# Scores of 64 attention units in plain float32 on half of TensorE's rows, in place of split operands on all rows

## The chip, the cores and the metric

The kernel runs on one core of a Trainium2 chip. A core has a matrix engine (TensorE, PE in the profile; PEld is its weight loading), VectorE (DVE), ScalarE (ACT), GpSimd (POOL) and SyncE (SP), which here issues the DMAs. Each engine runs its own list of instructions in order and waits for others through semaphores. Data lies in SBUF (128 partitions) and in PSUM, the output of TensorE, in eight banks of 512 float32 columns. The metric is the time of one execution on the device in microseconds (us).

## What is computed

Blockwise causal attention over q, k and v of 8 batches, 8 heads, 576 positions and 64 dimensions, and a feed-forward network on the result, all in float32:

```python
scores = scale * np.matmul(q, k.transpose(0, 1, 3, 2))  # scale = 1/8
mask = (pos[:, None] // 64) >= (pos[None, :] // 64)
scores = np.where(mask, scores, -1e9)
attn = np.exp(scores - scores.max(-1, keepdims=True))
attn = attn / (attn.sum(-1, keepdims=True) + 1e-9)
x = (attn @ v).transpose(0, 2, 1, 3).reshape(4608, 512)
h = x @ w_in                                                    # 512 x 2048
out = (h / (1 + np.exp(-h))) @ w_out                            # 2048 x 512
```

## The kernel before

**Float32 from a faster type.** TensorE takes plain float32 and float32r, a shorter type. Most matmuls here are float32r: an operand is split into a part `hi`, its cast to float32r, and a part `lo`, the rest, and a product is the sum of hi x hi, hi x lo and lo x hi. ScalarE does most of the casts and GpSimd the subtractions for `lo`.

**Units.** The first 128 query positions are handled early by other classes (`First`, L494, and `Second`, L551), whose scores are plain float32 matmuls with 64 rows of TensorE: `First.scores` at L526 uses four tiles of 64 rows by 64 output columns, one in each quarter, `Second.scores` at L578 two, one in the upper left and one in the lower right quarter. The other 448 queries of each of the 64 pairs of batch and head are a `Unit` (L263). A unit's keys are five tiles of 128, 128, 128, 128 and 64 positions; `SEG` (L40) has for each its number, its first column in the score buffer, its first query and how many queries see it: 448, 320, 192, 448 and 64 for the tiles 0, 2, 3, 1 and 4. `BANKS` (L45) puts tile 0 into PSUM bank 0, tiles 2 and 3 into bank 1, tiles 1 and 4 into bank 2.

**Steps of a unit, and their lines.** `load` (L269) brings q and k, transposed, with 64 dimensions as partitions, into the buffer `qkraw` twice by two DMAs, on partitions 0 to 63 and 64 to 127. `split_hi` (L278, ScalarE at L280) casts all of it to float32r into `qh`. `split_lo` (L282) overwrites the keys of `qh` on the partitions 64 to 127 by their rest (GpSimd, L284) and writes the rest of the queries to `ql` (GpSimd, L286). `scores` (L297) then contracts over all 128 partitions, so that one matmul adds the products with both parts of the keys: for each key tile two matmuls at L308, one with the queries' `qh` and one with `ql`, ten in all. `max` and `max2` (VectorE) find the maxima, `sub` subtracts them into the buffer `T`, `exp`, `p_hi` and `p_lo` make the weights and split them, `pv` (L382, matmuls at L387) multiplies with v, whose split `v_hi` and `v_lo` make, and `sums`, `lower`, `fold`, `mult`, `x_hi` and `x_lo` norm the result and split it into the FFN's input.

**FFN.** Blocks of 256 tokens: `ffn1` (L620) multiplies with w_in, `silu`, `g_hi` and `g_lo` (ScalarE, ScalarE, GpSimd) make the next operand, `ffn2` (L660) multiplies with w_out, all in float32r over 128 rows and 128 columns of TensorE.

**Order.** The schedule is written by hand. Up to unit 16 the string `ORDER` (L52) lists every step, a token like `u3.scores` being the method of unit 3 and `ffn` half a step of the FFN; from unit 17 on the loop at L760 does the same by rule: in its step i it issues the scores, `max` and `max2` of unit i, the splits of unit i+1, the load of unit i+2, some FFN, `pv` of unit i-1, and so on. Between a unit's matmuls TensorE always has FFN matmuls. SyncE issues all loads and stores in this order as well; a load waits until the buffer's former user is done. Every buffer named here exists once, so `qkraw` of unit i+2 is free when the splits of unit i+1 are done.

Of the kernel before, what the change touches and what calls it, by code (L numbers as in the profile page):

```python
# [9 lines left out]
F32 = mybir.dt.float32  # L10
F32R = mybir.dt.float32r
# [3 lines left out]
ALU = mybir.AluOpType  # L15
# [5 lines left out]
P = 128  # L21
NQ = S - 2 * D
# [17 lines left out]
SEG = [(0, 0, 0, 448), (2, 448, 128, 320), (3, 768, 256, 192), (1, 960, 0, 448), (4, 1408, 384, 64)]  # L40
COLS = 1472

QK = [0, 1, 3, 2, 4]
PV = [(0, 0, 128), (1, 0, 128), (2, 0, 128), (2, 1, 64), (1, 1, 64), (0, 1, 64), (4, 0, 128), (3, 1, 64), (3, 0, 128)]
BANKS = [(0, 448), (448, 960), (960, 1472)]  # L45

# [40 lines left out]
u2.sums u2.p_lo:2 u4.scores u1.mult g_lo u3.exp:0 ffn u3.exp:1 u4.max u5.split_hi u2.v_lo ffn u3.exp:2 u3.load_v u5.split_lo
u1.x_hi u3.sums u2.pv ffn silu u4.max2 u1.x_lo g_hi u6.load u2.lower ffn u3.p_hi:0 g_lo u3.v_hi u2.fold ffn u4.sub u3.v_lo silu
ffn u3.p_lo:0 u3.p_hi:1 u4.load_v g_hi u3.sums2 u3.p_hi:2 u3.p_lo:1 u5.scores u3.p_lo:2 ffn u4.exp:0 u5.max u6.split_hi g_lo u3.pv
u4.exp:1 u4.exp:2 u6.split_lo u5.max2 ffn u4.p_hi:0 u3.lower ffn u4.p_hi:1 u4.p_hi:2 u3.fold u4.p_lo:0 u7.load u5.sub ffn  # L90
u4.p_lo:1 silu ffn g_hi u3.mult u4.v_hi g_lo u6.scores u4.sums u3.x_hi u4.v_lo silu ffn u4.p_lo:2 u6.max u7.split_hi u5.load_v
store ffn u3.x_lo u6.max2 u4.pv u5.exp:0 u7.split_lo u5.exp:1 u5.exp:2 ffn u5.v_hi u5.sums u5.p_hi:0 u4.lower ffn u5.p_lo:0
u5.p_hi:1 u8.load u5.p_hi:2 u4.fold ffn g_hi u5.p_lo:1 u6.sub ffn u5.p_lo:2 u5.sums2 u6.exp:0 u7.scores u5.v_lo u6.exp:1 u6.exp:2
g_lo u6.load_v ffn u7.max u8.split_hi u5.pv u8.split_lo u7.max2 silu ffn g_hi u5.lower ffn u6.p_hi:0 g_lo u5.fold u9.load u6.v_hi
u7.sub u6.p_hi:1 ffn u6.v_lo silu u6.p_lo:0 g_hi ffn u7.load_v u5.mult u6.p_hi:2 g_lo u8.scores u6.sums u5.x_hi u6.p_lo:1 silu ffn
u9.split_hi u8.max u6.p_lo:2 ffn u5.x_lo u8.max2 u7.exp:0 u6.pv u7.exp:1 u9.split_lo u7.exp:2 ffn output g_hi u7.sums u7.v_hi ffn
u6.lower g_lo u7.p_hi:0 u10.load output u6.fold ffn u7.p_hi:1 u8.sub u7.p_lo:0 u7.p_hi:2 ffn u7.p_lo:1 u7.sums2 u9.scores
u7.p_lo:2 u8.exp:0 u8.exp:1 ffn u7.v_lo u9.max u8.exp:2 u10.split_hi u8.load_v u7.pv u10.split_lo u9.max2 ffn silu u7.lower ffn
# [34 lines left out]
def attn_ffn(ctx: ExitStack, tc: tile.TileContext, qk, v, qk0, v0, qk1, v1, w_in, w_out, out):  # L133
    nc = tc.nc
    pool = lambda name, bufs=1, **kw: ctx.enter_context(tc.tile_pool(name=name, bufs=bufs, **kw))
    cp = pool("const")
    sp = pool("work")
# [125 lines left out]
    class Unit:  # L263
# [3 lines left out]
            u.b, u.h, u.a = b, h, 64 * (h % 2)  # L267

        def load(u):  # L269
            u.raw = sp.tile([P, 1024], F32, tag="qkraw", name="qkraw")  # L270
            for r in (0, 64):
                nc.sync.dma_start(out=u.raw[r : r + 64], in_=qk[u.b, u.h])

        def load_v(u):
            u.vraw = sp.tile([P, 512], F32, tag="vraw", name="vraw")[:, : 5 * D]
            nc.sync.dma_start(out=u.vraw, in_=v[u.b, u.h])

        def split_hi(u):  # L278
            u.qh = sp.tile([P, 1024], F32R, tag="qh", name="qh")
            nc.scalar.copy(u.qh, u.raw)  # L280

        def split_lo(u):  # L282

            nc.gpsimd.tensor_tensor(out=u.qh[64:, NQ:], in0=u.raw[64:, NQ:], in1=u.qh[64:, NQ:], op=ALU.subtract)  # L284
            u.ql = sp.tile([P, 512], F32R, tag="ql", name="ql")[:, :NQ]
            nc.gpsimd.tensor_tensor(out=u.ql, in0=u.raw[:, :NQ], in1=u.qh[:, :NQ], op=ALU.subtract)  # L286
# [10 lines left out]
        def scores(u):  # L297
            banks = [bank(0), bank(1), bank(2)]

            def ps(c, w, r=P):  # L300
                i = max(i for i in range(3) if BANKS[i][0] <= c)
                return banks[i][:r, c - BANKS[i][0] : c - BANKS[i][0] + w]

            u.ps = ps
            for j, c, q0, w in (SEG[i] for i in QK):
                m = min(P, S - j * P)
                for i, qq in enumerate((u.qh, u.ql)):
                    nc.tensor.matmul(u.ps(c, w, m), u.kk[:, j * P : j * P + m], qq[:, q0 : q0 + w], start=i == 0, stop=i == 1)  # L308
# [118 lines left out]
    HALF = (slice(0, 64), slice(64, 128))  # L427
# [308 lines left out]
    units = [Unit(b, h) for b in range(B) for h in range(H)]  # L736
# [3 lines left out]
    a, b = First(0), First(1)  # L740
# [7 lines left out]
    for token in ORDER.split():  # L748
        name, _, method = token.partition(".")
# [10 lines left out]
    for i in range(TABLE, n + 2):  # L760
        u = units[i] if i < n else None
# [82 lines left out]
```

## Time and profile before

| | |
|---|---|
| median of 2 runs | 1041.92 us (1041.03 and 1042.81) |
| span of the profiled execution | 1040.4 us; its own total time is not given apart from the two runs |
| granted clock of TensorE | 1.000 |
| L308 to L308, scores of one unit to those of the next | some 12.7 us from 310 us on |
| DMA, mean over the span | 77 GB/s |

The profile is one execution recorded by the hardware. Times are microseconds from the start of the span, unless marked ns. L308 is line 308 of the kernel. In rows of groups stand the line, engine, operation, output and inputs by the program's names, the shapes, how many there were, then their busy time and the mean ns of one, then the idle time before them and what ended it. "128*64" is the part of TensorE used, rows by columns. In rows of the timeline stand the start, the time from the first start to the last end, and the count of like instructions merged. A plain float32 matmul shows as two weight loads and two matmuls. The ends of matmuls are modelled, and they overlap; their starts are recorded.

### The profile page before, as it was taken

How to read it: one execution, taken by the hardware profiler on the slowest of the kernel's cores; microseconds unless marked ns; L12 is line 12 of the kernel's file. 1: busy time of each engine (PE TensorE's matmuls, PEld its weight loads, DVE VectorE, ACT ScalarE, POOL GpSimd, SP SyncE). 2: the span in 40 equal slices, each digit the busy share in tenths (PEclk: the TensorE clock that was granted, in tenths of full speed). 3: DMA queues.
4: the chain of work that ended last, by engine and by line, in shares of the span. 5: the costliest groups of instructions: out<-in, count | busy, mean ns of one | idle time of the engine just before them, and what ended most of it. 6: DMA issues, size and time to landing. Idle time of an engine off the chain costs nothing.

```text
span 1040.4 us, 20218 instructions
## 1 busy us (share of the span) xinstructions
PE 1032.7 (99%) x7162; PEld 938.7 (90%) x7162; DVE 762.8 (73%) x2233; ACT 745.9 (72%) x1192; POOL 750.0 (72%) x726
## 2 busy tenths in 40 slices
PE   8999999999999999999999999999999999999998
PEld 8888899999999999999999999998999999989987
DVE  7998499999968988888878888888888888700000
ACT  4876498888987888787878787878787777722222
POOL 5775679988997878787878787878787878622221
PEclk9999999999999999999999999999999999999999
DMA  7865232232222222232222222222222222000000
GB/s 264 280 212 198 75 97 74 71 87 67 65 71 74 54 55 74 54 81 59 82 56 75 59 75 54 65 64 54 75 55 74 55 74 55 25 3 21 1 21 21
DMA packets 35188, 79.95 MB, mean 77 GB/s; under 512 B 4752, under 2 KB 13200, under 8 KB 35088
## 3 DMA queue, kind: packets, MB, share of 16 engines
q1 hardware_dynamic: 35088, 78.66, 27.2%
q8 instruction: 57, 0.93, 0.4%
q14 instruction: 43, 0.35, 0.1%
HBM read 69.21 MB, written 9.44 MB: 76 GB/s over the span
## 4 chain that ended last, share of the span: by engine, by line
PE 89%; POOL 4%; DVE 3%; DMA 1%; issue 1%; ACT 1%; SPq 0%; POOLq 0%; DVEq 0%; ACTq 0%
PE h L620 36%; PE o L660 36%; PE S L308 8%; PE U L387 8%; POOL pl L363 1%; DMA qk<-in_qk_dram 1%; PE S L660 1%; DVE wm L235 1%; PE S L578 1%; POOL qh L284 1%; DMA wst<-in_moe_w_out_dram 1%; POOL g L638 1%; DVE S L229 0%; POOL ql L286 0%; DVE S L225 0%
## 5 line engine op out<-in xcount | busy, mean ns | idle before, releaser
L620 PE MATMUL h<-x,wi 128*128 128x256 f32 x3456 | 441.0, 282 | 0.3 <-POOL x L424 0.3
L620 PEld LDWEIGHTS h<-x,wi 128*128 128x128 f32 x3456 | 430.0, 188 | 11.5 <-issue 0.5
L660 PE MATMUL o<-wo,g 128*128 128x512 f32 (+1 forms) x1680 | 423.9, 397 | 0.0
L660 PEld LDWEIGHTS o<-wo,g 128*128 128x128 f32 x1680 | 305.7, 188 | 62.6 <-issue 0.7
L363 POOL TENSOR_TENSOR pl<-p,ph 128x448 fp32r<-128x448 f32 (+1 forms) x192 | 226.0, 1202 | 92.9 <-ACT ph L355 92.9
L638 POOL TENSOR_TENSOR g<-g,g 128x512 fp32r<-128x512 f32 x144 | 186.4, 1294 | 120.3 <-ACT g L633 110.1
L252 DVE TRANSPOSE_TENSOR_REDUCE Mx<-S 64x4 f32<-64x128 f32 (+4 forms) x384 | 135.5, 405 | 92.9 <-PE S L308 92.7
L627 ACT ACTIVATE g<-h 128x512 f32<-128x512 f32 x144 | 86.1, 598 | 124.0 <-POOL g L638 76.3
L633 ACT CAST g<-g 128x512 fp32r<-128x512 f32 x144 | 89.3, 620 | 58.8 <-PE o L660 56.8
L252 DVE TRANSPOSE_TENSOR_REDUCE Dx<-p 128x14 f32<-128x448 f32 (+3 forms) x320 | 122.5, 445 | 0.1
L349 ACT ACTIVATE p<-T 128x512 f32<-128x512 f32 (+1 forms) x192 | 105.2, 604 | 14.8 <-POOL ph L365 13.8
L355 ACT CAST ph<-p 128x512 fp32r<-128x512 f32 (+1 forms) x192 | 104.1, 596 | 1.3 <-PE U L387 1.2
L284 POOL TENSOR_TENSOR qh<-qkraw,qh 64x576 fp32r<-64x576 f32 x64 | 91.8, 1434 | 16.6 <-ACT qh L280 7.7
L672 DVE TENSOR_TENSOR ot<-S,ot 128x256 f32<-128x256 f32 x1 | 0.4, 424 | 125.3 <-PE S L660 125.3
L308 PE MATMUL S<-qh 128*128 128x448 f32 (+3 forms) x320 | 91.1, 298 | 0.0
L627 ACT ACT_TABLE_LOAD x65 | 83.4, 1283 | 1.2
L308 PE MATMUL S<-ql,qh 128*128 128x448 f32 (+3 forms) x320 | 84.0, 307 | 0.0
L349 ACT ACT_TABLE_LOAD x61 | 78.3, 1283 | 1.3 <-DVE Dx L252 0.2
L286 POOL TENSOR_TENSOR ql<-qkraw,qh 128x448 fp32r<-128x448 f32 x64 | 74.1, 1158 | 5.0
L387 PE MATMUL U<-ph,vc 128*128 128x448 f32 (+3 forms) x320 | 74.0, 296 | 0.3 <-POOL vc L295 0.3
L340 DVE TENSOR_TENSOR T<-S,MR 128x256 f32<-128x256 f32 (+2 forms) x192 | 72.8, 405 | 0.0
L280 ACT CAST qh<-qkraw 128x1024 fp32r<-128x1024 f32 x64 | 66.9, 1045 | 7.3 <-DMA qkraw<-in_qk_dram 4.8
(121 smaller groups left out, 1175.3 us busy)
## 6 DMA issues: line engine op xcount, KB each, us to landing
qkraw<-in_qk_dram SPq DMA_DIRECT2D x128, 256.0 KB, 3.9
vraw<-in_v_dram SPq DMA_DIRECT2D x64, 160.0 KB, 2.3
wst<-in_moe_w_out_dram SPq DMA_DIRECT2D x15, 512.0 KB, 5.1
out_dram<-ot SPq DMA_DIRECT2D x23, 256.0 KB, 2.9
wst<-in_moe_w_in_dram SPq DMA_DIRECT2D x10, 512.0 KB, 5.4
out_dram<-ot SPq DMA_DIRECT2D x26, 128.0 KB, 2.4
v<-in_v_dram SPq DMA_DIRECT2D x12, 256.0 KB, 6.1
T<-in_moe_w_in_dram SPq DMA_DIRECT2D x6, 512.0 KB, 4.2
```

What stands on the lines that cost most here:

```text
L252: nc.vector.tensor_reduce(out=out, in_=in_, axis=AX.X, op=op, apply_transpose=True)
L284: nc.gpsimd.tensor_tensor(out=u.qh[64:, NQ:], in0=u.raw[64:, NQ:], in1=u.qh[64:, NQ:], op=ALU.subtract)
L308: nc.tensor.matmul(u.ps(c, w, m), u.kk[:, j * P : j * P + m], qq[:, q0 : q0 + w], start=i == 0, stop=i == 1)
L349: nc.scalar.activation(u.p[:, c:e], T[:, c:e], AF.Exp, scale=SCALE)
L355: nc.scalar.copy(u.ph[:, c:e], u.p[:, c:e])
L363: nc.gpsimd.tensor_tensor(out=u.pl[:, c:e], in0=u.p[:, c:e], in1=u.ph[:, c:e], op=ALU.subtract)
L387: nc.tensor.matmul(U[:m, q0 : q0 + w], u.vc[:, j, :m], (u.ph, u.pl)[pp][:, c : c + w], start=n == 0, stop=n == 8)
L620: nc.tensor.matmul(h[:, f, :], wi[wt][:, c, w], x[:, xt, :], start=n == 0, stop=n == 3 * CT - 1)
L627: nc.scalar.activation(g, hs.pop((blk, d)), AF.Silu)
L633: nc.scalar.copy(g2[:, 0], g)
L638: nc.gpsimd.tensor_tensor(out=g2[:, 1], in0=g, in1=g2[:, 0], op=ALU.subtract)
L660: nc.tensor.matmul(o, g2[:, gt, f, tk], wo[wt][:, 2 * d + f, c], start=(d == 0 or i > 0) and n == 0, stop=d == NSTEP - 1 and n == 5,)
```

## The change

The splits of q and k (`split_hi`, `split_lo`) are removed from the class, from `ORDER` and from the loop. `scores` issues one plain float32 matmul for each key tile, contracted over 64 partitions: key tiles 0, 1 and 4 on partitions 0 to 63, tiles 2 and 3 on partitions 64 to 127, each half reading its own copy of q and k as loaded. The order of the tiles, `QK`, goes from tiles 0, 2, 1, 3, 4 to 0, 2, 3, 1, 4. `load` alternates between the buffers `qkraw` (even heads) and `qh` (odd heads), as `qh` has no other use now. Nothing else in the order changes.

```diff
-QK = [0, 1, 3, 2, 4]
+QK = [0, 1, 2, 3, 4]
...
         def load(u):
-            u.raw = sp.tile([P, 1024], F32, tag="qkraw", name="qkraw")
+            u.raw = sp.tile([P, 1024], F32, tag=("qkraw", "qh")[u.h % 2], name="qkraw")
             for r in (0, 64):
                 nc.sync.dma_start(out=u.raw[r : r + 64], in_=qk[u.b, u.h])
...
-        def split_hi(u):
-            u.qh = sp.tile([P, 1024], F32R, tag="qh", name="qh")
-            nc.scalar.copy(u.qh, u.raw)
-
-        def split_lo(u):
-
-            nc.gpsimd.tensor_tensor(out=u.qh[64:, NQ:], in0=u.raw[64:, NQ:], in1=u.qh[64:, NQ:], op=ALU.subtract)
-            u.ql = sp.tile([P, 512], F32R, tag="ql", name="ql")[:, :NQ]
-            nc.gpsimd.tensor_tensor(out=u.ql, in0=u.raw[:, :NQ], in1=u.qh[:, :NQ], op=ALU.subtract)
-            u.kk = u.qh[:, NQ:]
...
             for j, c, q0, w in (SEG[i] for i in QK):
                 m = min(P, S - j * P)
-                for i, qq in enumerate((u.qh, u.ql)):
-                    nc.tensor.matmul(u.ps(c, w, m), u.kk[:, j * P : j * P + m], qq[:, q0 : q0 + w], start=i == 0, stop=i == 1)
+                a = HALF[j in (2, 3)]
+                nc.tensor.matmul(u.ps(c, w, m), u.raw[a, NQ + j * P : NQ + j * P + m], u.raw[a, q0 : q0 + w], start=True, stop=True)
...
         if i + 1 < n:
-            units[i + 1].split_hi()
-            units[i + 1].split_lo()
             if i + 2 < n:
                 units[i + 2].load()
```

In `ORDER` every token `u<k>.split_hi` and `u<k>.split_lo` is deleted, and no other token moves.

More of the change, by code (lines that the diff above doesn't have):

```diff
@@ L77 @@
 c2.sub:1 silu w31.bits:1 ffn w31.bits:2 w31.hi ffn w30.hi w31.lo c3.scores:0 w28.lo c2.exp ffn c3.max:0 g_hi c3.sub:0 c3.load_v
-ffn g_lo c2.sum u0.load c3.scores:1 w30.lo ffn c2.norm c3.max:1 c3.sub:1 ffn c3.exp c2.turn:0 ffn c3.sum c2.back:0 u0.split_hi
-c2.turn:1 ffn c3.norm c2.back:1 c2.pv silu c3.turn:0 g_hi u0.load_v ffn c3.back:0 g_lo c3.turn:1 ffn u0.split_lo c3.back:1 output
-c3.pv silu u0.v_hi c2.hi ffn mask g_hi u1.load c2.lo c3.hi g_lo ffn c3.lo u0.scores ffn u0.max u1.split_hi ffn silu u1.split_lo
@@ L81 @@
-g_hi u0.max2 ffn ffn u0.v_lo u0.sub ffn g_lo u1.load_v u2.load u1.scores silu store g_hi ffn g_lo u1.max u0.exp:0 ffn u2.split_hi
-u1.max2 ffn u0.exp:1 u2.split_lo u0.exp:2 output ffn u0.p_hi:0 u1.sub store u0.p_hi:1 ffn u0.p_hi:2 u0.p_lo:0 u3.load u0.sums
-u2.scores u0.p_lo:1 silu g_hi u0.p_lo:2 ffn u2.max ffn g_lo u1.exp:0 u3.split_hi u2.max2 u0.pv u1.exp:1 u3.split_lo u1.exp:2 ffn
+ffn g_lo c2.sum u0.load c3.scores:1 w30.lo ffn c2.norm c3.max:1 c3.sub:1 ffn c3.exp c2.turn:0 ffn c3.sum c2.back:0
@@ new lines @@
+c2.turn:1 ffn c3.norm c2.back:1 c2.pv silu c3.turn:0 g_hi u0.load_v ffn c3.back:0 g_lo c3.turn:1 ffn c3.back:1 output
+c3.pv silu u0.v_hi c2.hi ffn mask g_hi u1.load c2.lo c3.hi g_lo ffn c3.lo u0.scores ffn u0.max ffn silu
+g_hi u0.max2 ffn ffn u0.v_lo u0.sub ffn g_lo u1.load_v u2.load u1.scores silu store g_hi ffn g_lo u1.max u0.exp:0 ffn
+u1.max2 ffn u0.exp:1 u0.exp:2 output ffn u0.p_hi:0 u1.sub store u0.p_hi:1 ffn u0.p_hi:2 u0.p_lo:0 u3.load u0.sums
+u2.scores u0.p_lo:1 silu g_hi u0.p_lo:2 ffn u2.max ffn g_lo u1.exp:0 u2.max2 u0.pv u1.exp:1 u1.exp:2 ffn
@@ L84 @@
 u2.sub silu ffn u0.lower u4.load u1.p_hi:0 u1.sums ffn u1.p_hi:1 u1.p_lo:0 output g_hi u3.scores store u1.p_lo:1 u0.fold u1.v_hi
-output u1.sums2 u1.p_hi:2 ffn g_lo u4.split_hi ffn u1.p_lo:2 u3.max silu ffn u1.v_lo u4.split_lo u3.max2 u2.exp:0 u2.load_v u1.pv
+output u1.sums2 u1.p_hi:2 ffn g_lo ffn u1.p_lo:2 u3.max silu ffn u1.v_lo u3.max2 u2.exp:0 u2.load_v u1.pv
 u2.exp:1 u2.exp:2 ffn u2.p_hi:0 u3.sub u2.p_hi:1 u5.load u2.p_lo:0 ffn u1.lower g_hi u2.p_lo:1 u2.p_hi:2 u1.fold ffn u2.v_hi
-u2.sums u2.p_lo:2 u4.scores u1.mult g_lo u3.exp:0 ffn u3.exp:1 u4.max u5.split_hi u2.v_lo ffn u3.exp:2 u3.load_v u5.split_lo
+u2.sums u2.p_lo:2 u4.scores u1.mult g_lo u3.exp:0 ffn u3.exp:1 u4.max u2.v_lo ffn u3.exp:2 u3.load_v
@@ L88 @@
 u1.x_hi u3.sums u2.pv ffn silu u4.max2 u1.x_lo g_hi u6.load u2.lower ffn u3.p_hi:0 g_lo u3.v_hi u2.fold ffn u4.sub u3.v_lo silu
-ffn u3.p_lo:0 u3.p_hi:1 u4.load_v g_hi u3.sums2 u3.p_hi:2 u3.p_lo:1 u5.scores u3.p_lo:2 ffn u4.exp:0 u5.max u6.split_hi g_lo u3.pv
-u4.exp:1 u4.exp:2 u6.split_lo u5.max2 ffn u4.p_hi:0 u3.lower ffn u4.p_hi:1 u4.p_hi:2 u3.fold u4.p_lo:0 u7.load u5.sub ffn
-u4.p_lo:1 silu ffn g_hi u3.mult u4.v_hi g_lo u6.scores u4.sums u3.x_hi u4.v_lo silu ffn u4.p_lo:2 u6.max u7.split_hi u5.load_v
@@ L92 @@
-store ffn u3.x_lo u6.max2 u4.pv u5.exp:0 u7.split_lo u5.exp:1 u5.exp:2 ffn u5.v_hi u5.sums u5.p_hi:0 u4.lower ffn u5.p_lo:0
+ffn u3.p_lo:0 u3.p_hi:1 u4.load_v g_hi u3.sums2 u3.p_hi:2 u3.p_lo:1 u5.scores u3.p_lo:2 ffn u4.exp:0 u5.max g_lo u3.pv
+u4.exp:1 u4.exp:2 u5.max2 ffn u4.p_hi:0 u3.lower ffn u4.p_hi:1 u4.p_hi:2 u3.fold u4.p_lo:0 u7.load u5.sub ffn
+u4.p_lo:1 silu ffn g_hi u3.mult u4.v_hi g_lo u6.scores u4.sums u3.x_hi u4.v_lo silu ffn u4.p_lo:2 u6.max u5.load_v
+store ffn u3.x_lo u6.max2 u4.pv u5.exp:0 u5.exp:1 u5.exp:2 ffn u5.v_hi u5.sums u5.p_hi:0 u4.lower ffn u5.p_lo:0
@@ L93 @@
 u5.p_hi:1 u8.load u5.p_hi:2 u4.fold ffn g_hi u5.p_lo:1 u6.sub ffn u5.p_lo:2 u5.sums2 u6.exp:0 u7.scores u5.v_lo u6.exp:1 u6.exp:2
-g_lo u6.load_v ffn u7.max u8.split_hi u5.pv u8.split_lo u7.max2 silu ffn g_hi u5.lower ffn u6.p_hi:0 g_lo u5.fold u9.load u6.v_hi
+g_lo u6.load_v ffn u7.max u5.pv u7.max2 silu ffn g_hi u5.lower ffn u6.p_hi:0 g_lo u5.fold u9.load u6.v_hi
 u7.sub u6.p_hi:1 ffn u6.v_lo silu u6.p_lo:0 g_hi ffn u7.load_v u5.mult u6.p_hi:2 g_lo u8.scores u6.sums u5.x_hi u6.p_lo:1 silu ffn
-u9.split_hi u8.max u6.p_lo:2 ffn u5.x_lo u8.max2 u7.exp:0 u6.pv u7.exp:1 u9.split_lo u7.exp:2 ffn output g_hi u7.sums u7.v_hi ffn
+u8.max u6.p_lo:2 ffn u5.x_lo u8.max2 u7.exp:0 u6.pv u7.exp:1 u7.exp:2 ffn output g_hi u7.sums u7.v_hi ffn
@@ L97 @@
 u6.lower g_lo u7.p_hi:0 u10.load output u6.fold ffn u7.p_hi:1 u8.sub u7.p_lo:0 u7.p_hi:2 ffn u7.p_lo:1 u7.sums2 u9.scores
-u7.p_lo:2 u8.exp:0 u8.exp:1 ffn u7.v_lo u9.max u8.exp:2 u10.split_hi u8.load_v u7.pv u10.split_lo u9.max2 ffn silu u7.lower ffn
+u7.p_lo:2 u8.exp:0 u8.exp:1 ffn u7.v_lo u9.max u8.exp:2 u8.load_v u7.pv u9.max2 ffn silu u7.lower ffn
 g_hi u7.fold u8.p_hi:0 g_lo u11.load u8.p_hi:1 u9.sub ffn u8.p_lo:0 silu ffn u7.mult g_hi u8.p_lo:1 u8.p_hi:2 u10.scores u8.sums
-u8.v_hi u8.p_lo:2 u7.x_hi ffn u11.split_hi u10.max u8.v_lo ffn u7.x_lo u9.load_v store u10.max2 u9.exp:0 u8.pv u11.split_lo
+u8.v_hi u8.p_lo:2 u7.x_hi ffn u10.max u8.v_lo ffn u7.x_lo u9.load_v store u10.max2 u9.exp:0 u8.pv
@@ L101 @@
 u9.exp:1 u9.exp:2 ffn u9.p_hi:0 u9.sums u9.p_hi:1 ffn g_lo u8.lower u12.load u9.v_hi u8.fold ffn u9.v_lo u10.sub u9.p_lo:0
 u10.load_v ffn silu u9.p_lo:1 g_hi u9.sums2 u9.p_hi:2 u11.scores u9.p_lo:2 ffn u10.exp:0 u11.max u10.exp:1 g_lo u10.exp:2 u9.pv
-u12.split_hi u11.max2 ffn u9.lower u12.split_lo u10.p_hi:0 ffn u9.fold u11.sub silu ffn u10.p_lo:0 g_hi u13.load u10.p_hi:1 ffn
+u11.max2 ffn u9.lower u10.p_hi:0 ffn u9.fold u11.sub silu ffn u10.p_lo:0 g_hi u13.load u10.p_hi:1 ffn
 g_lo u10.v_hi u10.sums u10.p_hi:2 u12.scores u10.p_lo:1 silu u9.mult g_hi u10.v_lo ffn u12.max u10.p_lo:2 u11.load_v u11.exp:0 ffn
-store u11.exp:1 g_lo u9.x_hi u12.max2 u10.pv u11.exp:2 u9.x_lo u13.split_hi ffn u10.lower u11.sums u13.split_lo u11.p_hi:0 ffn
+store u11.exp:1 g_lo u9.x_hi u12.max2 u10.pv u11.exp:2 u9.x_lo ffn u10.lower u11.sums u11.p_hi:0 ffn
@@ L106 @@
 u11.p_hi:1 u11.p_hi:2 u10.fold u11.v_hi ffn u12.sub u11.p_lo:0 u14.load ffn silu u11.v_lo u11.sums2 u13.scores u11.p_lo:1
-u12.load_v u11.p_lo:2 u12.exp:0 ffn g_hi u13.max u12.exp:1 u14.split_hi g_lo ffn u12.exp:2 u13.max2 u14.split_lo u11.pv ffn silu
+u12.load_v u11.p_lo:2 u12.exp:0 ffn g_hi u13.max u12.exp:1 g_lo ffn u12.exp:2 u13.max2 u11.pv ffn silu
 g_hi u13.sub u11.lower ffn u15.load g_lo u12.p_hi:0 u12.p_hi:1 u11.fold ffn u12.p_lo:0 u12.sums silu u12.v_hi u12.p_lo:1
-u14.scores u12.p_hi:2 output u11.mult u12.p_lo:2 ffn store u14.max u13.exp:0 u12.v_lo ffn u11.x_hi u15.split_hi u13.load_v
@@ L110 @@
-u11.x_lo u14.max2 u12.pv u13.exp:1 u13.exp:2 u15.split_lo ffn output u13.p_hi:0 u13.sums u12.lower ffn g_hi u13.p_hi:1 g_lo
+u14.scores u12.p_hi:2 output u11.mult u12.p_lo:2 ffn store u14.max u13.exp:0 u12.v_lo ffn u11.x_hi u13.load_v
+u11.x_lo u14.max2 u12.pv u13.exp:1 u13.exp:2 ffn output u13.p_hi:0 u13.sums u12.lower ffn g_hi u13.p_hi:1 g_lo
 u12.fold u13.v_hi ffn u16.load u13.p_hi:2 u14.sub u13.p_lo:0 ffn u13.p_lo:1 u13.sums2 silu u15.scores u13.p_lo:2 ffn u14.exp:0
-u15.max u13.v_lo g_hi u14.exp:1 ffn g_lo u16.split_hi u14.load_v u15.max2 u13.pv u14.exp:2 u16.split_lo ffn silu u15.sub
+u15.max u13.v_lo g_hi u14.exp:1 ffn g_lo u14.load_v u15.max2 u13.pv u14.exp:2 ffn silu u15.sub
@@ L115 @@
 g_hi ffn g_lo u14.lower u15.sums u15.p_hi:0 ffn u15.p_hi:1 u15.p_lo:0 u15.v_hi u15.p_hi:2 u14.fold ffn u15.v_lo u16.sub u15.p_lo:1
-u16.load_v ffn silu store u17.split_hi u15.p_lo:2 u15.sums2 ffn u17.split_lo u15.pv u16.exp:0 u16.exp:1 ffn g_hi u16.exp:2 g_lo
+u16.load_v ffn silu store u15.p_lo:2 u15.sums2 ffn u15.pv u16.exp:0 u16.exp:1 ffn g_hi u16.exp:2 g_lo
 u15.lower u18.load ffn u16.p_hi:0 u15.fold u16.p_hi:1 u16.p_lo:0 u16.v_hi u15.mult ffn u16.v_lo ffn silu u16.p_lo:1 u17.load_v
```

## The prediction

> **What bounds the kernel now.** First the page: span, busy times, slices, chain.
>
> ```profile
> span 1040.4 us, 20218 instructions
> PE 1032.7 (99%) x7162; PEld 938.7 (90%) x7162; DVE 762.8 (73%) x2233; ACT 745.9 (72%) x1192; POOL 750.0 (72%) x726
> PE   8999999999999999999999999999999999999998
> PEclk9999999999999999999999999999999999999999
> PE 89%; POOL 4%; DVE 3%; DMA 1%; issue 1%; ACT 1%; SPq 0%; POOLq 0%; DVEq 0%; ACTq 0%
> ```
>
> TensorE is busy 99% of the span at the full clock, every other engine under 75%, and 89% of the chain is TensorE. An average can hide stages, so next the busy times by window:
>
> ```profile
> 120.00:200.00 80.00, 80.00 (x516) 73.06 (x515) 73.35 (x235) 63.09 (x100) 65.59 (x63) 1.00 0.33 82
> 310.00:720.00 410.00, 410.00 (x2652) 374.52 (x2652) 341.24 (x1064) 325.33 (x516) 328.88 (x323) 1.00 0.25 64
> 720.00:890.00 170.00, 169.70 (x1102) 155.06 (x1101) 139.75 (x437) 134.78 (x215) 134.01 (x134) 1.00 0.25 64
> PE U L387 <- POOL vc L295: 0.3, 1, 0.3
> ```
>
> The columns are window, length, then busy time of PE, PEld, DVE, ACT, POOL. Over the stretch with the 64 units TensorE has no gap to give back: 410.00 of 410 us. The last row, of the waits, is the one wait of TensorE for GpSimd there. So a unit costs the kernel what its matmuls occupy on TensorE, and the change is judged there alone.
>
> One unit's scores now, from the timeline (start, duration), and two rows of the chain for the pace of the FFN around them:
>
> ```profile
> 508.21 0.39 PE L660 MATMUL o<-wo,g 128*128 128x512 f32 x1
> 508.44 0.36 PE L308 MATMUL S<-qh 128*128 128x448 f32 x1
> 509.56 0.25 PE L308 MATMUL S<-qh 128*128 128x192 f32 x1
> 509.65 0.28 PE L308 MATMUL S<-ql,qh 128*128 128x192 f32 x1
> 509.76 0.19 PE L308 MATMUL S<-qh 128*64 128x64 f32 x1
> 509.79 0.22 PE L308 MATMUL S<-ql,qh 128*64 128x64 f32 x1
> 509.84 0.36 PE L620 MATMUL h<-x,wi 128*128 128x256 f32 x1
> 509.84 0.48 PE L620 MATMUL h<-x,wi 128*128 128x256 f32 x2
> 521.12 0.37 PE L308 MATMUL S<-qh 128*128 128x448 f32 x1
> 505.79 2.81 PE o L660 x12
> 524.15 2.82 PE h L620 x24
> ```
>
> Durations overlap, so starts are what counts. FFN matmuls follow one another at 2.81/12 = 0.234 us (L660) and 2.82/24 = 0.1175 us (L620). Entry into the scores: 508.21 to 508.44 is 0.23, no loss. The ten matmuls: 508.44 to 509.84, 1.40. Behind them the second L620 starts at 510.04 (the pair ends at 510.32, one takes 0.28), 0.20 after the first instead of 0.12: 0.08 lost. One unit now: 1.48 us.
>
> **The change part by part.**
>
> *Plain float32 scores.* Ten matmuls of 128 rows become five of 64 rows. The trace has no plain float32 matmul of 64 rows by 128 columns; nearest are L578 (64 by 64 tiles, moving 128 columns, two halves by turns) and L526 (all four quarters). L578 issues 64 calls:
>
> ```profile
> L578 PE MATMUL S<-qk 64*64 64x128 f32 x128 | 8.7, 275 | 0.6 <-DVE x L604 0.3 <-issue 0.3
> L578 PEld LDWEIGHTS S<-qk 64*64 64x64 f32 x128 | 6.8, 132 | 2.7 <-issue 1.2 <-DVE x L604 1.1
> L308 PEld LDWEIGHTS S<-qh 128*128 128x128 f32 x256 | 48.1, 188 | 3.8
> 33.91 0.60 PE L578 MATMUL S<-qk 64*64 64x128 f32 x8
> 34.02 0.49 PE L578 MATMUL S<-qk 64*64 64x128 f32 x6
> 34.13 0.39 PE L578 MATMUL S<-qk 64*64 64x128 f32 x4
> 34.23 0.28 PE L578 MATMUL S<-qk 64*64 64x128 f32 x2
> 100.67 0.28 PE L620 MATMUL h<-x,wi 128*128 128x256 f32 x1
> 100.88 0.33 PE L578 MATMUL S<-qk 64*64 64x128 f32 x2
> 101.90 0.39 PE L620 MATMUL h<-x,wi 128*128 128x256 f32 x1
> 101.90 0.51 PE L620 MATMUL h<-x,wi 128*128 128x256 f32 x2
> ```
>
> 128 instructions for 64 calls: two passes a call. The rows from 33.91 on are the same stretch from later and later starts, two instructions fewer each time: a pair, one on each half, starts every (34.23 - 33.91)/3 = 0.107 us. So a pass holds its half 0.107/128 = 0.84 ns a column, and the halves run side by side. After the change the lower half has key tiles 0, 1 and 4: (448 + 448 + 64) x 2 passes x 0.84 = 1.605 us. The upper half has tiles 2 and 3: (320 + 192) x 2 x 0.84 = 0.856 us, hidden beside it (on the path if the halves don't overlap). With QK = 0, 1, 2, 3, 4 the order is tile 0, 2, 3, 1, 4, and the upper half's outputs lie in bank 1, the lower half's in banks 0 and 2.
>
> *Changing the tile.* Around L578 the pace breaks. Entry: 100.67 to 100.88 is 0.21 for an L620 that takes 0.1175 of pace, 0.09 lost. Block: 100.88 to 101.90 is 1.02 for eight pairs at 0.107, 0.165 lost (the first weight load and the way out). After: the second L620 starts at 101.90 + 0.51 - 0.28 = 102.13, 0.23 after the first, 0.11 lost. Together 0.365 us. The new block's first weights have 128 columns, not 64: 0.188 - 0.132, another 0.055. The Trainium skill ("TensorEngine Tiling", Key Properties) says that a change of tiling mode, not merely of the tile, drains TensorE. L578 agrees with its 0.09; tile 3 to tile 4 above, 509.65 to 509.76 with 0.02 lost, does not. Without that sentence the sum is the same.
>
> *Tile 4 has 64 output columns*, so the tile changes once more inside the block. Low bound: the 0.02 of tile 3 to tile 4 now (0.11 against the 0.09 from 509.56 to 509.65), float32r on both sides. High: a whole switch over again, 0.365. Between them, entry and first load of L578: if the way out takes 0.09 as the way in does, 0.165 leaves 0.07 for the first load, so 0.09 + 0.07 = 0.16. One row has the same step in columns, the other the same type; I take the middle of these two, 0.09.
>
> *Sum.* 1.605 + 0.365 + 0.055 + 0.09 = 2.115 us, less 1.48: 0.635 us a unit, x 64 = 40.6 us.
>
> *The splits go.*
>
> ```profile
> L280 ACT CAST qh<-qkraw 128x1024 fp32r<-128x1024 f32 x64 | 66.9, 1045 | 7.3 <-DMA qkraw<-in_qk_dram 4.8 <-PE S L308 2.0
> L284 POOL TENSOR_TENSOR qh<-qkraw,qh 64x576 fp32r<-64x576 f32 x64 | 91.8, 1434 | 16.6 <-ACT qh L280 7.7 <-issue 3.1 <-POOL g L638 1.2
> L286 POOL TENSOR_TENSOR ql<-qkraw,qh 128x448 fp32r<-128x448 f32 x64 | 74.1, 1158 | 5.0
> qkraw<-in_qk_dram SPq DMA_DIRECT2D x128, 256.0 KB, 3.9
> ```
>
> ScalarE loses 66.9 us, GpSimd 91.8 + 74.1 = 165.9 us. All of it lay beside TensorE; what can come back is TensorE's waiting, the 0.3 us quoted and, by an estimate from the 0.3 us without busy time between 720 and 890 us, about as much elsewhere: 0.5 us. If GpSimd had been late at every unit this would be the main term; the windows say that it was not.
>
> *Loads.* The same 128 DMAs, now by turns into two buffers. TensorE waits for them itself, with FFN matmuls queued behind. A load for unit i+2 is issued in step i, waits on SyncE's queue for the scores of unit i (done earlier in that step; v loads and stores stand behind it), lands in 3.9 us, and is read two steps later. A step is one unit's share of the stretch, 521.12 - 508.44 = 12.7 us (the next unit's scores start at 521.12, above), so the cover is about 20 us: cost nothing. VectorE's maximum waits for scores that take 0.6 us longer, in a step that grows as much: nothing.
>
> **Total.** Against the profiled execution: 1040.4 + 40.6 - 0.5 = 1080.5 us of span. The two runs shown stand 0.6 and 2.4 us over that span, the median 1.5; so 1082 us. The forecast's own range: 0.02 for tile 4 and no 0.055 gives 0.51 us a unit, 1074; 0.365 for tile 4 gives 0.91, 1100.
>
> **Rivals.**
>
> *Switches cost what tile 3 to tile 4 costs now (not slower).* If entry, tile 4 and exit lose 0.02 each, with weights loaded ahead, and 0.08 behind them stays, a unit takes 1.605 + 0.06 + 0.08 = 1.745, 0.265 more: 17 us, 1058 us, within 2%. It decides below (20.8 + 0.5)/64 = 0.33 us a unit. For it: that step now. Against: L578's entry and exit.
>
> *TensorE starts matmuls only in their written order.* Each call's two passes stand in a row, so tile 2 could start only with tile 0's second pass at 0.373, tile 3's second at 1.067, and tile 1 not before, though its half is free at 0.747; the end is 1.92 instead of 1.605: +20 us, 1102 us. The Trainium skill ("TensorE: Matmul & The Clock Gate", What overlaps and what doesn't) states that matmuls start and end strictly in program order, which would lead there. Against it, L526, whose calls go round the quarters:
>
> ```profile
> 5.08 0.37 PE L526 MATMUL S<-qk 64*64 64x64 f32 x1
> 5.09 0.37 PE L526 MATMUL U<-qk 64*64 64x64 f32 x1
> 5.09 0.37 PE L526 MATMUL S<-qk 64*64 64x64 f32 x1
> 5.10 0.37 PE L526 MATMUL U<-qk 64*64 64x64 f32 x1
> 5.24 0.31 PE L526 MATMUL S<-qk 64*64 64x64 f32 x1
> ```
>
> Four calls, S and U by turns, start within 0.02 us, before any second pass. By the trace the rule does not hold here.
>
> *The halves do not overlap with 128 output columns each.* The 0.856 us come onto the path: +55 us, 1137 us. L526 speaks against it: its S and U calls come from different row halves and write the same partitions of two banks at once.
>
> **How the numbers follow.** Forecast 0.75 (its range holds about nine tenths of it), no-loss switches 0.10, written order 0.08, no overlap 0.05, something unseen 0.02. The range 1066 to 1104 takes in the forecast's and the written-order rival, about 0.8; what is left out is 1058 and 1137. Two per cent, about what a measurement tells from no change, is 1062.8 us: slower 0.89, within 0.10, faster 0.01.
>
> **What the profile after would show.** Starts at L308's new line: first pass to next FFN matmul about 1.9 us (1.40 now); tile 2's first pass within 0.02 us of tile 0's; tile 1's first pass about 0.75 us in, not 1.07; 0.09 lost at entry; ACT near 679 and POOL near 584 us busy, TensorE still without gaps from 310 us on. I am wrong if a unit's scores take 1.6 us or 2.4, or if TensorE waits for qkraw or qh loads.

## The result and the profile after

| | before | after |
|---|---|---|
| median of 2 runs | 1041.92 us | 1083.78 us (1082.59 and 1084.97) |
| ratio to before | 1 | 1.0403, 95% interval 1.0368 to 1.0439 |
| span of the profiled execution | 1040.4 us | 1083.2 us |
| granted clock of TensorE in it | 1.000 | 0.998 |

The change makes the kernel 4% slower; 1082 us was forecast. One run below, of the kernel without the rests, took 1245.35 us at a granted clock of 0.753 and is not in its ratio. The page of the changed kernel, the lines that answer to those shown of before; L297 is the new line of the scores, L609 and L649 are the FFN lines that were L620 and L660:

```profile
span 1083.2 us, 19821 instructions
PE 1076.0 (99%) x7162; PEld 921.3 (85%) x7162; DVE 759.0 (70%) x2233; ACT 687.4 (63%) x1128; POOL 585.2 (54%) x598
PE 95%; DVE 2%; DMA 1%; issue 0%; POOL 0%; ACT 0%; SPq 0%; DVEq 0%; ACTq 0%
L649 PE MATMUL o<-wo,g 128*128 128x512 f32 (+1 forms) x1680 | 424.5, 398 | 0.0
L297 PE MATMUL S<-qkraw 64*128 64x448 f32 (+3 forms) x640 | 129.4, 434 | 0.0
```

GpSimd lost 750.0 - 585.2 = 164.8 us of work and ScalarE 58.5, and the kernel grew all the same: the chain that ended last is now 95% TensorE, and GpSimd's share of it went from 4% to 0%. There are as many matmul instructions as before, 7162: ten passes a unit replace ten matmuls.

Busy time by window (window, length, then PE, PEld, DVE, ACT, POOL), first of before, then of after:

```profile
200.00:310.00 110.00, 109.67 (x711) 100.29 (x710) 98.64 (x309) 96.17 (x158) 99.30 (x101) 1.00 0.29 73
```

```profile
200.00:310.00 110.00, 110.00 (x672) 92.57 (x673) 102.88 (x321) 82.83 (x141) 70.88 (x76) 1.00 0.26 67
310.00:720.00 410.00, 410.00 (x2526) 346.98 (x2524) 313.55 (x987) 283.34 (x463) 231.92 (x245) 1.00 0.24 63
720.00:930.00 210.00, 210.00 (x1290) 178.05 (x1290) 165.04 (x521) 143.28 (x235) 120.17 (x129) 1.00 0.22 58
```

In 410 us TensorE did 2526 matmuls where it had done 2652, without a gap in either. The third of a microsecond that it had waited between 200 and 310 us is gone, and so is the 0.30 us between 720 and 890 us (170 less 169.70, in the windows of before). The second was a wait for GpSimd too, by the waits of before (engine, line waited for, total us, times, longest):

```profile
PE h L620 <- POOL x L424: 0.3, 1, 0.3
```

That makes 0.6 us in all; there was no more to win.

Where the 42.8 us of span came from shows in the first and last starts of the scores' matmuls (the view of one source line: count, min/median/max duration, first and last start), before and after:

```profile
L308 PE MATMUL S<-qh x320: 192/307/375, 121.6 to 890.8; 128*128 128x448 f32 x64, 128*64 128x64 f32 x32, 128*128 128x320 f32 x32, 128*128 128x192 f32 x32
```

```profile
L297 PE MATMUL S<-qkraw x640: 218/481/640, 123.0 to 933.5; 64*128 64x448 f32 x64, 64*128 64x192 f32 x32, 64*64 64x64 f32 x32, 64*128 64x320 f32 x32
```

From the first to the last score 769.2 us became 810.5: 41.3 us over 63 steps and the longer last block. Another 1.4 us lie ahead of the first score, where the change takes away only the splits of the first units. TensorE's waits there, before and after:

```profile
PE o L526 <- DMA qk<-in_qk_dram: 0.9, 2, 0.6
```

```profile
PE o L515 <- DMA qk<-in_qk_dram: 2.5, 2, 2.2
```

The first loads of the program held TensorE up for 1.6 us longer in this execution. Its granted clock (the third number from the end) was lower as well in the first 20 us, and 1.00 in every later window:

```profile
0.00:20.00 20.00, 17.33 (x352) 16.46 (x352) 12.42 (x20) 7.30 (x10) 9.43 (x15) 1.00 0.86 315
```

```profile
0.00:20.00 20.00, 16.42 (x295) 15.78 (x296) 10.74 (x18) 5.66 (x7) 8.54 (x14) 0.91 0.86 314
```

Of the kernels below, the one with all key tiles on one half has both again (0.91, and 2.1 us of this wait) and reaches its first score at 122.5 us. The others have 1.00 and at most 0.8 us of the wait, and reach it between 120.3 and 121.6 us; two of them differ from the changed kernel in the order of the key tiles alone. So the 1.4 us are chance of the execution; whether the late loads or the clock bring them is not shown. TensorE waits for no load of a unit, neither qkraw nor qh, anywhere.

One unit after, from several small windows of the timeline (start, time to the last end, count; each row is the group of one window and begins with the matmul that was the first still running there):

```profile
358.90 0.28 PE L609 MATMUL h<-x,wi 128*128 128x256 f32 x1
359.11 0.64 PE L297 MATMUL S<-qkraw 64*128 64x448 f32 x2
359.59 0.91 PE L297 MATMUL S<-qkraw 64*128 64x448 f32 x4
359.97 1.11 PE L297 MATMUL S<-qkraw 64*128 64x448 f32 x3
360.34 0.79 PE L297 MATMUL S<-qkraw 64*128 64x448 f32 x3
360.81 0.32 PE L297 MATMUL S<-qkraw 64*64 64x64 f32 x2
360.92 0.22 PE L297 MATMUL S<-qkraw 64*64 64x64 f32 x1
361.06 0.50 PE L649 MATMUL o<-wo,g 128*128 128x512 f32 x1
361.06 0.73 PE L649 MATMUL o<-wo,g 128*128 128x512 f32 x2
```

Two passes are in flight from 359.11 on: tile 0 on the lower half and tile 2 on the upper. Tile 0's second pass starts 0.48 later (0.375 of streaming and 0.105 for the first weights), tile 1's passes at 359.97 and 360.34, tile 4's at 360.81 and 360.92, the FFN at 361.06: 1.95 us, where the block took 1.40. The second FFN matmul starts at 361.06 + 0.73 - 0.40 (the mean of L649 above) = 361.39, 0.33 after the first instead of 0.234: 0.10 lost. The upper half is never seen on the path.

### The profile page after: what moved, and what is told of

It reads as the page before. It is cut to its first block, busy times and chain, and to the rows that moved or that the text cites. A ratio compares the mean times of both kernels' runs of the same rounds, so it can differ in the third digit from the quotient of the medians.

```text
span 1083.2 us, 19821 instructions
## 1 busy us (share of the span) xinstructions
PE 1076.0 (99%) x7162; PEld 921.3 (85%) x7162; DVE 759.0 (70%) x2233; ACT 687.4 (63%) x1128; POOL 585.2 (54%) x598
## 4 chain that ended last, share of the span: by engine, by line
PE 95%; DVE 2%; DMA 1%; issue 0%; POOL 0%; ACT 0%; SPq 0%; DVEq 0%; ACTq 0%
PE h L609 37%; PE o L649 36%; PE S L297 12%; PE U L376 8%; DMA qk<-in_qk_dram 1%; PE S L649 1%; PE idle L425 1%; DMA wst<-in_moe_w_out_dram 1%; PE S L567 1%; DVE wm L235 1%; DVE S L229 1%; DVE S L225 0%; PE S L585 0%; PE S L467 0%; POOL MR L460 0%
## 5 line engine op out<-in xcount | busy, mean ns | idle before, releaser
L609 PE MATMUL h<-x,wi 128*128 128x256 f32 x3456 | 441.5, 282 | 0.0
L609 PEld LDWEIGHTS h<-x,wi 128*128 128x128 f32 x3456 | 430.0, 188 | 13.2 <-issue 0.5
L649 PE MATMUL o<-wo,g 128*128 128x512 f32 (+1 forms) x1680 | 424.5, 398 | 0.0
L649 PEld LDWEIGHTS o<-wo,g 128*128 128x128 f32 x1680 | 305.4, 188 | 64.9 <-issue 0.5
L252 DVE TRANSPOSE_TENSOR_REDUCE Mx<-S 64x4 f32<-64x128 f32 (+4 forms) x384 | 130.0, 402 | 133.8 <-PE S L297 133.5
L297 PE MATMUL S<-qkraw 64*128 64x448 f32 (+3 forms) x640 | 129.4, 434 | 0.0
L297 PEld LDWEIGHTS S<-qkraw 64*128 64x128 f32 (+1 forms) x640 | 72.4, 175 | 64.2 <-issue 51.6
L284 POOL TENSOR_TENSOR vc<-vraw,vc 128x320 fp32r<-128x320 f32 x64 | 56.5, 882 | 70.5 <-ACT vc L281 69.7
L281 ACT CAST vc<-vraw 128x320 fp32r<-128x320 f32 x64 | 29.5, 460 | 66.7 <-PE U L376 64.6
L376 PEld LDWEIGHTS U<-ph,vc 128*128 128x128 f32 x320 | 58.1, 189 | 4.5
```

The costliest lines, as they stand in the source:

```text
L252: nc.vector.tensor_reduce(out=out, in_=in_, axis=AX.X, op=op, apply_transpose=True)
L297: nc.tensor.matmul(u.ps(c, w, m), u.raw[a, NQ + j * P : NQ + j * P + m], u.raw[a, q0 : q0 + w], start=True, stop=True)
L376: nc.tensor.matmul(U[:m, q0 : q0 + w], u.vc[:, j, :m], (u.ph, u.pl)[pp][:, c : c + w], start=n == 0, stop=n == 8)
L609: nc.tensor.matmul(h[:, f, :], wi[wt][:, c, w], x[:, xt, :], start=n == 0, stop=n == 3 * CT - 1)
L649: nc.tensor.matmul(o, g2[:, gt, f, tk], wo[wt][:, 2 * d + f, c], start=(d == 0 or i > 0) and n == 0, stop=d == NSTEP - 1 and n == 5,)
```

## The experiments

Ratios are to the kernel before, timed on the same chip in the same stretch. The changed kernel itself was not run again there; the run with the old order of key tiles has the same block, takes the same 810.5 us from the first to the last score (120.7 to 931.2 us), and stands in for it at 1082.59 us.

### Tile 4 without a change of tile

```diff
-                m = min(P, S - j * P)
...
-                nc.tensor.matmul(u.ps(c, w, m), u.raw[a, NQ + j * P : NQ + j * P + m], u.raw[a, q0 : q0 + w], start=True, stop=True)
+                nc.tensor.matmul(u.ps(c, w), u.raw[a, NQ + j * P : NQ + j * P + P], u.raw[a, q0 : q0 + w], start=True, stop=True)
...
-        "qk": np.concatenate([qT[..., 2 * D :], kT], axis=-1),
+        "qk": np.concatenate([qT[..., 2 * D :], kT, kT[..., 4 * P :]], axis=-1),
```

The buffers `qkraw` and `qh` grow to 1088 columns for it.

> The changed kernel (1083.8 us), with tile 4 given 128 key columns (its 64 keys, and the same once more, loaded behind them), so that its matmul has the same 64 by 128 tile as the others; the second copy's scores land on unused rows. My theory: the step from tile 1 to tile 4 costs about 0.145 us a unit (0.09 before the first weights can be loaded, 0.055 for the load) and goes; the way out stays: 1083.8 - 64 x 0.145 = 1074.5 us. Rival, the step is as cheap as that from tile 3 to tile 4 in the kernel before (0.02 us): 1082.5 us.

Measured: 1077.46 us, ratio 1.0344 (1.0326 to 1.0361): 5.1 us less than the old order's 1082.59, four times what the rival gives, and little over half of my 9.3. Matmuls of one block from the timeline, and below them the one weight load that answers for tile 4's second pass:

```profile
355.05 1.77 PE L296 MATMUL S<-qkraw 64*128 64x448 f32 x8
356.28 0.70 PE L296 MATMUL S<-qkraw 64*128 64x448 f32 x3
356.71 0.27 PE L296 MATMUL S<-qkraw 64*128 64x64 f32 x1
356.91 0.49 PE L648 MATMUL o<-wo,g 128*128 128x512 f32 x1
```

```profile
356.66 0.19 PEld L296 LDWEIGHTS S<-qkraw 64*128 64x128 f32 x1 [0.19 <-issue]
```

Tile 1's second pass starts at 356.28 and takes 0.375; tile 4's first begins with the load of the weights for its second, at 356.66, so the step costs nothing now. It had cost 360.81 - 360.34 - 0.375 = 0.095, and its first weights another 0.055 (360.81 to 360.92 is 0.11 for a pass of 64 columns, 0.053 at the pace of the others). That part of the theory holds. But the block is 356.91 - 355.05 = 1.86 us, only 0.09 less than 1.95: the way out takes 356.91 - 356.71 - 0.053 = 0.15, where the changed kernel has 361.06 - 360.92 - 0.053 = 0.09. Why that is, the last experiment asks.

### All key tiles on one half

```diff
-                a = HALF[j in (2, 3)]
+                a = HALF[0]
```

> The changed kernel with all five key tiles on the lower half of the rows. My theory: tiles 2 and 3 now lie beside the others, and come onto the path with (320 + 192) x 2 passes x 0.836 ns = 0.856 us a unit: 1083.8 + 54.8 = 1138.6 us. Rival, the halves do not really run at once (starts in the trace are only issue times): no change, 1083.8 us.

Measured: 1141.0 us, ratio 1.0953 (1.0931 to 1.0975), 58.4 us more than the old order's 1082.59. Some 1.8 us of that lie ahead of the first score (122.5 against 120.7 us). From the first to the last score the kernel takes 866.9 us (122.5 to 989.4) against 810.5, 56.4 more, 0.88 us a unit, where 0.856 was worked out. The chain (start, length, count), this kernel first, then the changed one:

```profile
376.28 2.82 PE S L297 x10
```

```profile
359.18 1.95 PE S L297 x8
```

The block on the chain is 2.82 us where it was 1.95, longer by 0.87, which is what had lain beside it. The halves do run at once, with 128 output columns each.

### The lower half's tiles written first, and the old order

```diff
-QK = [0, 1, 2, 3, 4]
+QK = [0, 3, 1, 2, 4]
```

> The changed kernel with the key tiles written in the order 0, 1, 2, 3, 4, so that four passes of the lower half stand ahead of tile 2. My theory, each half takes its own next pass however it is written: tile 2's first pass still starts with tile 0's, 1083.8 us. Rival 1, matmuls start in written order: tile 2 starts with tile 1's second pass at about 1.23 us of the block, the upper half ends at 2.09 instead of 1.7: about +0.38 us a unit, 1108 us. Rival 2, TensorE looks past one waiting pass of a half but not past two or three: tile 2 starts when tile 1's first pass does, at 0.86 us, the upper half ends at 1.71, as the lower one does: 1084 to 1086 us, and only the starts tell.

```diff
-QK = [0, 1, 2, 3, 4]
+QK = [0, 1, 3, 2, 4]
```

> The changed kernel with the key tiles in their old order 0, 2, 1, 3, 4, which undoes that part of the change. My theory: no change, 1083.8 us, with tile 3's first pass at 0.65 us of the block as now, ahead of tile 1's at 0.86, or at the latest together with tile 1's; the upper half ends by 1.2 us in either case, well before the lower one. Rival, written order: tile 3 starts with tile 1's second pass at 1.23 us and ends at 1.55, still before tile 1: the same time, so only the starts tell.

Measured: 1082.7 us (ratio 1.0394, 1.0378 to 1.0409) and 1082.59 us (1.0393, 1.0377 to 1.0408). The time does not depend on the order. That alone would not refute a look past one waiting pass; the start does. With the lower half's four passes written ahead of tile 2 (first row: the FFN; second: the window from 356.47 to 356.60; third: one of the groups of that window):

```profile
356.26 0.28 PE L609 MATMUL h<-x,wi 128*128 128x256 f32 x1
356.47 0.64 PE L297 MATMUL S<-qkraw 64*128 64x448 f32 x2
L297 PE MATMUL S<-qkraw 64*128 64x320 f32 x1 | 0.5, 533 | 0.0
```

Two passes are in flight within 0.13 us of the block's start, and one of them has the 320 columns of tile 2, though tile 0's second pass and both of tile 1 stand ahead of it in the written order. The trace's rows agree with neither a written order nor a look past a single pass. With the old order, tile 3 (192 columns) is in flight by 357.50 to 357.55, 0.65 us into a block that starts at 356.85, as expected; tile 1, written ahead of it, starts at 0.86:

```profile
L297 PE MATMUL S<-qkraw 64*128 64x192 f32 x1 | 0.3, 322 | 0.0
```

The reordering of `QK` in the change is worth nothing. The rule of the Trainium skill weighed in the prediction ("TensorE: Matmul & The Clock Gate", What overlaps and what doesn't: matmuls start in program order) does not hold between row halves here.

### The splits as dead work, and the rests left out alone

To the changed kernel, at the places that `split_hi` and `split_lo` had (for unit 0 both stand where its `split_lo` stood):

```diff
+        def split_hi(u):
+            u.ql = sp.tile([P, 512], F32R, tag="ql", name="ql")
+            for i in range(2):
+                nc.scalar.copy(u.ql, u.raw[:, 512 * i : 512 * i + 512])
+
+        def split_lo(u):
+            for i in range(2):
+                nc.gpsimd.tensor_tensor(out=u.ql, in0=u.raw[:, 512 * i : 512 * i + 512], in1=u.ql, op=ALU.subtract)
```

> The changed kernel with work of the splits' size put back at their old places in the order, on ScalarE (two casts of 128 by 512 a unit) and GpSimd (two subtractions of 128 by 512), its results used by nothing. My theory: all of that lies beside TensorE's work, so the removed splits brought at most the 0.5 us I took for them: 1084 to 1085 us. Rival, the freed engines paid back a part of what the plain float32 scores cost: 1090 us or more.

And to the kernel before:

```diff
-            nc.gpsimd.tensor_tensor(out=u.qh[64:, NQ:], in0=u.raw[64:, NQ:], in1=u.qh[64:, NQ:], op=ALU.subtract)
-            u.ql = sp.tile([P, 512], F32R, tag="ql", name="ql")[:, :NQ]
-            nc.gpsimd.tensor_tensor(out=u.ql, in0=u.raw[:, :NQ], in1=u.qh[:, :NQ], op=ALU.subtract)
+            u.ql = u.qh[:, :NQ]
```

> The kernel before (1041.9 us) without GpSimd's two subtractions: the scores' ten float32r matmuls take the cast keys on all rows and the cast queries in both passes. It leaves out the rests of q and k. My theory: 165.9 us less work on GpSimd bring at most the wait of TensorE near 270 us, 1041.0 to 1041.9 us. Rival, GpSimd's share of the chain of work, 4% of the span, was worth time: 1035 us or less.

Measured: 1082.98 us (ratio 1.04, 1.0384 to 1.0415) with the dead work, as without it, and again 810.5 us from the first to the last score (121.6 to 932.1); 1041.83 us (ratio 1.0003, 0.9993 to 1.0013) without the rests, as before. The busy times of the first, by window:

```profile
310.00:720.00 410.00, 410.00 (x2522) 346.89 (x2521) 314.05 (x987) 317.90 (x525) 310.57 (x306) 1.00 0.24 62
```

GpSimd is back at 310.57 of 410 us (231.92 in the changed kernel) and TensorE does not notice. The work that the change removes was worth nothing: GpSimd's part by both runs, ScalarE's casts by the dead work alone. So the 4% that the change costs is all the scores' own.

### One more change of tile

```diff
                 nc.tensor.matmul(u.ps(c, w, m), u.raw[a, NQ + j * P : NQ + j * P + m], u.raw[a, q0 : q0 + w], start=True, stop=True)
+                if j == 3:
+                    nc.tensor.matmul(banks[0][:, NQ:], wi[0][:, 0, :P], wi[0][:, 0, P : P + 64], start=True, stop=True)
```

> The changed kernel with one more matmul, float32r over the whole array, 64 moving columns into unused columns of a bank, between key tiles 3 and 1: TensorE leaves the half-row tile and comes back once more in each unit. My theory: it must wait for both halves (0.97 us of the block), drain 0.09, load weights 0.11, run 0.03, drain 0.09, load tile 1's weights 0.11, so that tile 1 starts streaming at about 1.40 instead of 0.86: +0.54 us a unit, 1118 us. Rival, a change of tile costs next to nothing (0.02 each time) and the block's extra lies elsewhere: the wait for both halves, 0.03 and 0.04, about +0.19 us a unit, 1096 us.

Measured: 1118.46 us, ratio 1.0739 (1.0718 to 1.0761), 35.9 us more than the old order's 1082.59, or 0.56 us a unit. From the timeline, tile 3's second pass, the added matmul, and tile 1's two passes:

```profile
368.48 0.32 PE L297 MATMUL S<-qkraw 64*128 64x192 f32 x1
368.73 0.30 PE L299 MATMUL S<-wi 128*128 128x64 f32 x1
368.96 0.64 PE L297 MATMUL S<-qkraw 64*128 64x448 f32 x1
369.44 0.79 PE L297 MATMUL S<-qkraw 64*128 64x448 f32 x3
```

Tile 3's pass streams until 368.64 (192 columns, 0.16); the full matmul starts 0.09 later. It streams 0.03, after 0.11 for its weights, and tile 1 starts at 368.96, again 0.09 later; its second pass follows after 0.48, not 0.375: weights once more. So each change here between the full array and half rows is a drain of 0.09 and a first load of 0.11.

### Tile 4 with 128 columns, but not last

```diff
-QK = [0, 1, 2, 3, 4]
+QK = [0, 1, 2, 4, 3]
```

> The kernel of e1_tile4_wide (tile 4 with 128 key columns) with tile 4 written ahead of tile 1 and not last. In e1 the block ended 0.088 us earlier than in the changed kernel, not 0.145: from tile 4's last pass to the next FFN matmul it lost 0.148 us (1.717 to 1.865 of the block) where the changed kernel loses 0.095. Theory: a load of 128 key columns takes about 0.11 us and a pass of 64 moving columns hides only 0.053 of it, so the second pass really streams 0.054 us later than its start says, and the loss goes with the short passes: it comes twice (into tile 4's second pass and into tile 1's first) and the way out loses only 0.095: block 1.92 us, 1.865 + 0.054, and 3.5 us more than e1, about 1081 us. Rival: leaving a tile of 128 columns costs 0.148 us whatever stood last: block 1.865 us, 1077.5 us as e1.

Measured: 1081.61 us, ratio 1.0388 (1.037 to 1.0405), 4.2 us more than with tile 4 last. From the timeline: the block's first two passes, tile 1's first pass alone, its second alone with the FFN behind it:

```profile
356.28 0.64 PE L296 MATMUL S<-qkraw 64*128 64x448 f32 x2
357.30 0.59 PE L296 MATMUL S<-qkraw 64*128 64x448 f32 x1
357.73 0.54 PE L296 MATMUL S<-qkraw 64*128 64x448 f32 x1
358.20 0.50 PE L648 MATMUL o<-wo,g 128*128 128x512 f32 x1
```

The block is 358.20 - 356.28 = 1.92 us, as the theory gave. The way out is 358.20 - 357.73 - 0.375 = 0.095 again, and the loss has moved: tile 1's first pass takes 0.43 to its second, not 0.375. A load of 128 key columns does not fit beside a pass of 64 moving columns, whichever tile follows.

Not tried: balancing the halves, with a part of tile 1 on the upper one (736 columns each), as then both halves would write into PSUM bank 2 with nothing to order them. By the pace of 0.836 ns it would save 224 x 2 x 0.836 = 0.375 us a unit, an estimate from these rows. With tile 4's step gone too, a block of 1.95 - 0.375 - 0.09 = 1.485 us and 0.20 around it still exceed the 1.48 us of the kernel before. No version tried here beats the kernel before.

## Why the prediction was right, point by point

- **What bounds the kernel.** Right: TensorE without gaps in the stretch with units, and dead work on the other engines changes nothing (1082.98 us).
- **Streaming of the plain float32 passes.** Right: tile 1's two passes start 360.34 - 359.97 = 0.37 us apart for 448 columns, 0.84 ns a column.
- **The halves side by side.** Right: 0.88 us a unit is what it costs when they are not; 0.856 was the row's price. The two rivals against it are refuted, no overlap by that run, the written order by the starts.
- **Entry, first weights, way out.** Right within 0.03 us: 0.09 at entry (358.90 to 359.11, less 0.1175), first weights 0.105 where 0.07 + 0.055 was taken, 0.095 on the way out, 0.10 behind it where 0.11 was taken. Tile 1's first pass starts 0.86 us into the block (359.97), not at the 0.75 named as a sign: that figure left out the first weights, which the sum had. The added change of tile confirmed the sum, +0.56 us where 0.54 was expected.
- **Tile 4.** The term of the sum too small: 0.15 (a drain of 0.095 and 0.055 for weights) where the middle of 0.02 and 0.16 was taken. The two ends stood for two mechanisms, almost no cost or drain and load, and the middle for neither; the runs show the second, and the row of tile 3 to tile 4 in float32r was no guide. That is 0.06 us a unit, 3.8 us. First weights smaller by 0.02 give back 1.3.
- **Splits and loads at nothing.** Right: 0.5 us was taken, and the two waits of TensorE that went made 0.6. The prediction called the 0.3 us at L387 the one wait for GpSimd in the stretch; the other 0.3, at L620, was one too. No load of a unit delays TensorE. ScalarE ended at 687 us busy, not 679, without effect.
- **The sum.** 0.09 + 1.95 + 0.10 is 2.14 us against 2.115, so 0.66 us a unit more than the 1.48 before, 42.2 us. The two executions differ by 42.8, but 1.4 of these came ahead of the first score by chance; the 41.4 that are left are 0.65 us a unit, 0.01 less than the block's rows give, and of these 0.8 us in all the waits that went are 0.6. The forecast of 1082 us, 1.8 us under the median, is closer than its terms: tile 4 was 3.8 us too small, the weights 1.3 too large, and one of the two runs has the 1.4 us of chance.

## What to carry to other kernels

When one engine has no gaps, a change is worth what it does to that engine alone, however much it takes off the others: here 223 us of their work went for nothing. Two row halves of TensorE do run at once, but a plain float32 matmul is two passes of 0.84 ns a column (float32r took 0.09 us for 192 columns, 0.47 ns), so with unequal halves (960 and 512 columns) the longer one is the price, and a block of a few hundred columns pays for each change of tile as well. Before giving a small matmul at the end of such a block a tile of its own, look whether its weights can be loaded beside the pass ahead of it.

## What the runs showed of the hardware beyond that

- TensorE picks the next pass of each half for itself, past at least three waiting passes of the other: tile 2 started with tile 0 though both passes of tile 1 and tile 0's second stood ahead of it.
- The recorded start of a pass can be earlier than its streaming: in the kernel with tile 4 widened its second pass starts 0.05 us after the first, as if nothing were late, and the 0.05 us that its weights still lack appear behind it, in the way out (0.15 instead of 0.095) or in the next pass. Losses are better read from the second start behind a suspect than from its own.
- The step from 128 to 64 output columns cost a drain of 0.095 us in plain float32 on 64 rows and about 0.02 us in float32r on 128 rows. The number of rows does not decide it, by two steps of the kernel before in plain float32 on all 128 rows: the last two passes of a run of transposes (L478) and the matmuls of zeros behind them (L436), then an FFN matmul and the first of L596:

```profile
18.16 0.38 PE L478 MATMUL S<-ident,p 128*128 128x128 f32 x2
18.27 0.27 PE L478 MATMUL S<-ident,p 128*128 128x128 f32 x1
18.47 0.33 PE L436 MATMUL idle<-zero 128*64 128x64 f32 x2
117.35 0.28 PE L620 MATMUL h<-x,wi 128*128 128x256 f32 x1
117.56 0.27 PE L596 MATMUL S<-p,v 128*64 128x64 f32 x1
```

  L436 starts 0.20 us behind a pass whose pace is 0.11 (18.16 to 18.27), and L596 0.21 behind one whose pace is 0.1175: 0.09 lost both times. So between type and rows, the type is what these rows leave.
